# Waiting for six stores instead of 120 semaphores at the end of a kernel on SyncE

## The chip, the cores and the metric

The kernel runs on one core of one Trainium2 chip. The metric is the device time of one execution in microseconds (us). A profile of one execution goes with it: it has every instruction of the five engines, TensorE (PE), VectorE (DVE), ScalarE (ACT), GpSimd (POOL) and SyncE (SP), and the packets of the DMA engines.

## The reference

The input `x` has 2048 tokens of 512 channels. The output is a gated sum of two branches over the same input:

```
g   = sigmoid((x * gate_w).sum(-1))
a   = A(x)      # attention with a compressive memory, 32 heads, 4 segments of 512 tokens
b   = B(x)      # state-space layer: each channel convolved with its own kernel of length 2048
out = g * a + (1 - g) * b
```

Branch A projects `x` to queries, keys and values, takes causal softmax attention inside each segment, mixes it with a read from a memory that is summed up over the earlier segments, and multiplies the result by `wo`. Branch B builds, for each channel, a kernel of length 2048 from 128 complex modes and convolves the channel's 2048 values with it. The output is bf16, 2048 x 512.

## The kernel before

The kernel is a graph of operations with the order of their execution written out. `op` (line 164) records one operation with its engine, what it reads and writes, and the operations that it depends on; `dma` (line 223) records a transfer, nearly always on SyncE's queue. In the profile every plain transfer therefore has line 225, every scaled copy from PSUM line 232 or 233, and every matrix product line 706. `replay` takes the written-out order and gives each buffer (a tile) its slot in a pool; an operation that writes a slot used earlier also depends on the operations that last used the slot.

`emit` (line 267) turns this into five instruction streams. Every transfer counts a semaphore up by 16 when it has landed. There are 120 such semaphores (`NDMA` is 150, and 30 are left out), given out in turn, so that with some 257 transfers each of them is used two or three times. `emit` then goes through the operations in order and works out which waits each one needs. It keeps, for every engine, what that engine already knows: if it has waited for an operation, it knows all that this operation knew when it ran. A wait for something known is left out. `o.know` is what is known to whoever has waited for operation `o`, and `last[e]` what engine `e` knows after its last operation.

The work ends in `finals` (line 1503), which makes 16 blocks of 128 x 512 outputs. Matrix products gather both branches in PSUM; ScalarE or VectorE scales each block into half of an output tile; and every second block a transfer stores the tile, 256 KB, to the output in memory. That makes eight stores, all on SyncE, out of a pool of output tiles:

```
ouP = mkpool("ou", 2048, 6, 2)                        # line 685: six buffers
```

The pool has six buffers, so the seventh and the eighth tile take the buffers of the first and the second, and the copies that write them wait for those two stores.

When a SyncE stream has run through its operations, lines 339 to 342 add waits: one for each semaphore that any transfer has counted, to its final value. Then the block ends: each engine has a jump out of its stream and a DRAIN, and the engines meet, with GpSimd in the middle. The profile shows these under line 1603, where the block is closed.

Of the kernel before, what the change touches and what calls it, by code (L numbers as in the profile page):

```python
# [98 lines left out]
class Sched:  # L99
# [167 lines left out]
    def emit(self):  # L267
        nc, es = self.nc, self.es
        sems = {e: es.enter_context(nc.semaphore("q_" + e)) for e in ("PE", "ACT", "DVE", "POOL")}
        npool = sum(o.isdma for o in self.prog["POOL"])  # L270
        nhw = NDMA - npool if npool > 20 else NDMA - 30
        dsem = [es.enter_context(nc.semaphore("d%d" % i)) for i in range(nhw + npool)]
        block = es.enter_context(nc.Block())
        duse = [None] * len(dsem)
        dcnt = [0] * len(dsem)
        nd = nsw = 0
        last = {e: {} for e in self.prog}
        for o in self.order:
            know = dict(last[o.eng])
            o.waits = []  # L280
            deps = {id(d): d for d in o.alld}
            if o.isdma:
                if o.eng == "POOL":
                    k = nhw + nsw
                    nsw += 1
                else:
                    k = nd % nhw
                    nd += 1
                if duse[k] is not None:
                    deps[id(duse[k])] = duse[k]  # L290
                duse[k] = o
                dcnt[k] += 1
                o.sem, o.val = ("D", k), dcnt[k]
            else:
                o.sem, o.val = o.eng, o.idx
            o.inc = False
            for d in sorted(deps.values(), key=lambda d: -d.pos):
                assert d.pos < o.pos
                if d.eng == o.eng and o.eng == "PE":
                    continue  # L300
                if know.get(d.sem, 0) >= d.val:
                    continue
                o.waits.append(d)
                d.inc = True
                for kk, vv in d.know.items():
                    if know.get(kk, 0) < vv:
                        know[kk] = vv
            last[o.eng] = know
            o.know = dict(know)
            o.know[o.sem] = max(o.know.get(o.sem, 0), o.val)  # L310
        cum = {}
        for e, lst in self.prog.items():
            n = 0
            for o in lst:
                if not o.isdma and o.inc:
                    n += 1
                cum[id(o)] = n

        def tok(d):
            if d.isdma:  # L320
                return dsem[d.sem[1]], 16 * d.val
            return sems[d.eng], cum[id(d)]

        def make(e):
            def run(eng):
                for o in self.prog[e]:
                    need = {}
                    for d in o.waits:
                        s, v = tok(d)
                        if id(s) not in need or need[id(s)][1] < v:  # L330
                            need[id(s)] = (s, v)
                    for s, v in need.values():
                        eng.wait_ge(s, v)
                    ins = o.fn(eng)
                    if o.isdma:
                        ins.then_inc(dsem[o.sem[1]], 16)
                    elif o.inc:
                        ins.then_inc(sems[e], 1)
                if e == "SP":
                    for k in range(len(dsem)):  # L340
                        if dcnt[k]:
                            eng.wait_ge(dsem[k], 16 * dcnt[k])
            return run
        with nc.allow_low_precision("bf16 kernel by design"):
            block.sync(make("SP"))
            block.tensor(make("PE"))
            block.scalar(make("ACT"))
            block.vector(make("DVE"))
            block.gpsimd(make("POOL"))
# [1299 lines left out]
```

## Time and profile before

| | us |
|---|---|
| time, three runs | 289.74, 290.23, 293.19 |
| median | 290.23 |
| span of the profiled execution | 287.5 |
| busy in the span: VectorE, ScalarE, TensorE | 265.0, 254.6, 253.1 |
| last store of the output issued | 283.04 |
| waits of line 342 on SyncE: count, first and last start | 60, 283.4 and 287.0 |

The span runs from the first to the last instruction of the profiled execution. Of this execution's time the profile has no other figure than the span; the times of the table come from runs without a profile. Engines' busy times count what they compute. Instructions that only wait, jump, or issue a transfer belong to an engine's sequencer (marked q behind the engine's name) and count as nothing there; they have a start and a duration of their own all the same, and a line of the kernel. The duration of a wait instruction does not include the time that it stood waiting: its start is the time at which it could go on. A transfer is listed with the instruction that issued it, and its landing is the time at which its semaphore has its full count.

### The profile page before, as it was taken

What the parts mean: (1) busy time and instruction counts of PE and PEld (TensorE: products, weight loads), DVE (VectorE), ACT (ScalarE), POOL (GpSimd) and SP (SyncE); (2) the same over time, 40 slices, a digit from 0 to 9 for tenths busy, and PEclk for the clock granted to TensorE, in tenths of its full rate; (3) what the DMA queues carried; (4) which work ended last, traced back from release to release, by engine and by line L of the source; (5) the groups of instructions that cost most, each with busy time, mean ns of one, the idle gap of its engine ahead of it and who ended that gap; (6) DMA issues with size and microseconds to landing.
All of it is one profiled execution on the core that took longest, in us unless ns stands there. A gap on an engine that the chain in (4) does not pass through costs nothing.

```text
span 287.5 us, 9336 instructions
## 1 busy us (share of the span) xinstructions
PE 253.1 (88%) x3896; PEld 158.7 (55%) x3947; DVE 265.0 (92%) x617; ACT 254.6 (89%) x320; POOL 5.0 (2%) x10
## 2 busy tenths in 40 slices
PE   5767888787898989979999989999999999999992
PEld 2424454564556546756766657665555454555661
DVE  3998999999999999979999999999999999997782
ACT  5998999999999999989989999999999999983212
POOL 5000000000000000000000000000000000000000
PEclk9999899999999999979999999999999999999999
DMA  6996762421125256914643388585776795894224
GB/s 164 270 223 143 184 203 84 130 87 42 41 47 134 63 141 205 226 32 97 188 132 102 90 252 244 166 232 161 234 215 168 207 229 160 243 186 102 72 109 182
DMA packets 60187, 44.49 MB, mean 155 GB/s; under 512 B 36209, under 2 KB 53490, under 8 KB 60146
## 3 DMA queue, kind: packets, MB, share of 16 engines
q1 hardware_dynamic: 60146, 43.90, 57.0%
q8 instruction: 31, 0.51, 0.8%
q14 instruction: 10, 0.08, 0.1%
HBM read 22.09 MB, written 7.86 MB: 104 GB/s over the span
## 4 chain that ended last, share of the span: by engine, by line
ACT 35%; PE 28%; DVE 26%; issue 5%; DMA 3%; SPq 0%; DVEq 0%; ACTq 0%
PE psum L706 28%; ACT sb L1237 10%; ACT sb L229 10%; ACT sb L1190 8%; DVE sb L1346 7%; DVE sb L1355 3%; ACT sb L850 3%; DVE sb L230 2%; DMA sb<-sb 2%; DVE sb L1349 2%; DVE sb L1487 2%; DVE sb L1358 2%; DVE sb L1249 1%; DVE sb L1154 1%; ACT sb L1021 1%
## 5 line engine op out<-in xcount | busy, mean ns | idle before, releaser
L706 PE MATMUL psum<-sb 128*128 128x17 bf16 (+17 forms) x3808 | 247.4, 229 | 23.5 <-ACT sb L1190 7.4
L706 PEld LDWEIGHTS psum<-sb 128*128 128x128 bf16 (+6 forms) x3859 | 153.5, 102 | 115.5 <-issue 20.7
L229 ACT ACTIVATE sb<-psum 128x512 bf16<-128x512 f32 (+4 forms) x155 | 87.7, 624 | 7.6 <-PE psum L706 6.4
L1237 ACT ACTIVATE sb<-psum 128x2048 bf16<-128x2048 f32 x40 | 76.0, 1899 | 2.1 <-PE psum L706 1.7
L1190 ACT ACTIVATE sb<-psum 128x2048 bf16<-128x2048 f32 (+1 forms) x40 | 70.1, 1751 | 2.8 <-PE psum L706 2.7
L1346 DVE TENSOR_TENSOR sb<-sb 128x4096 bf16<-128x4096 bf16 (+3 forms) x24 | 37.7, 1569 | 0.0
L230 DVE CAST sb<-psum 128x512 bf16<-128x512 f32 (+1 forms) x49 | 29.9, 626 | 1.1 <-PE psum L706 0.9
L1355 DVE TENSOR_TENSOR sb<-sb 128x512 bf16<-128x512 bf16 (+1 forms) x48 | 25.0, 537 | 0.1
L1249 DVE TENSOR_TENSOR sb<-sb 128x1024 bf16<-128x1024 bf16 (+1 forms) x40 | 22.6, 577 | 0.2
L1487 DVE TENSOR_TENSOR sb<-sb 128x1024 bf16<-128x1024 bf16 x32 | 21.6, 685 | 0.9 <-ACT sb L229 0.5
L1349 DVE TENSOR_TENSOR sb<-sb 128x2048 bf16<-128x2048 bf16 (+3 forms) x24 | 20.7, 861 | 0.0
L232 ACT ACTIVATE sb<-psum,sb 128x512 bf16<-128x512 f32 x6 | 4.0, 687 | 12.3 <-PE psum L706 12.3
L1154 DVE TENSOR_TENSOR sb<-psum,sb 128x256 bf16<-128x256 f32 x32 | 13.3, 417 | 0.3
L1358 DVE TENSOR_TENSOR sb<-sb 128x512 bf16<-128x512 bf16 (+1 forms) x24 | 12.9, 536 | 0.0
L850 ACT ACTIVATE sb<-sb 128x512 f32<-128x512 f32 x18 | 11.8, 660 | 0.0
L1151 DVE RECIPROCAL sb<-psum 128x16 f32<-128x16 f32 x32 | 7.9, 252 | 1.8 <-PE psum L706 1.7
L1291 DVE TENSOR_TENSOR sb<-psum,sb 128x512 bf16<-128x512 f32 x12 | 8.2, 687 | 0.2
L858 ACT ACTIVATE sb<-sb 128x512 bf16<-128x512 f32 x12 | 8.0, 683 | 0.0
L1072 ACT ACTIVATE sb<-sb 128x512 bf16<-128x512 bf16 x12 | 8.0, 663 | 0.0
L1021 ACT ACTIVATE sb<-psum 128x512 bf16<-128x512 bf16 x12 | 7.8, 646 | 0.0
L852 DVE SCALAR_TENSOR_TENSOR sb<-sb 128x256 f32<-128x256 f32 x18 | 7.5, 424 | 0.0
L851 DVE TENSOR_TENSOR sb<-sb 128x256 f32<-128x256 f32 x18 | 7.5, 423 | 0.0
(78 smaller groups left out, 122.3 us busy)
## 6 DMA issues: line engine op xcount, KB each, us to landing
sb<-sb SPq DMA_DIRECT2D x64, 128.0 KB, 3.2
sb<-c_DN SPq DMA_DIRECT2D x32, 224.0 KB, 3.0
scr_Z<-sb SPq DMA_DIRECT2D x16, 256.0 KB, 3.2
sb<-scr_Z SPq DMA_DIRECT2D x16, 256.0 KB, 3.6
sb<-in_A_x_dram SPq DMA_DIRECT2D x5, 512.0 KB, 4.6
sb<-c_DN SPq DMA_DIRECT2D x16, 160.0 KB, 3.3
out_dram<-sb SPq DMA_DIRECT2D x8, 256.0 KB, 2.1
scr_O<-sb SPq DMA_DIRECT2D x12, 128.0 KB, 2.7
```

Source lines behind the costliest of these rows:

```text
L229: fa = lambda e: e.activation(dst(), src(), ACT.Copy)
L230: fd = lambda e: e.tensor_copy(dst(), src())
L706: mm = lambda e, o_, l, r_, st, sp, **kw: e.matmul(o_, lhsT=l, rhs=r_, start=st, stop=sp, skip_group_check=True, **kw)
L850: op("ACT", ("As", 512), lambda e, sq=sq, Z=Z: e.activation(ap(sq, n=512), ap(Z, n=512), ACT.Square), r=[Z], w=[sq], key=PW[h] + PWS * k)
L1190: o = op("ACT", ("Ax", 4 * n), lambda e: e.activation(ap(pT, dims=[[512, 4], [1, n]]), ap(P, dims=[[512, 4], [1, n]]), ACT.Exp, scale=0.25 ...
L1237: o = op("ACT", ("Ax", 2048), lambda e, P=P, pT=pT: e.activation(ap(pT, n=2048), ap(P, n=2048), ACT.Exp, scale=0.25), r=[P], w=[pT])
L1249: op("DVE", ("V2", 128 * nb), lambda e, pT=pT, dims=dims: e.tensor_tensor(ap(pT, dims=dims + [[1, 128]]), ap(pT, dims=dims + [[1, 128]]), ...
L1346: op("DVE", ("V2n1" if n == 1 else "V2", 512 * n), lambda e: e.tensor_tensor(ap(tile, 2 * dst, [[2 * (sp - dst), 2], [2 * ne, 128], [1, 2 ...
L1349: op("DVE", ("V2n1" if n == 1 else "V2", 256 * n), lambda e: e.tensor_tensor(D_(), D_(), ap(tile, 2 * sp + ne * 128, [[-ne * 128, 2], [2 * ...
L1355: op("DVE", ("V2x" if sstep > 2 else "V2", 256 * n), lambda e, half=half: e.tensor_tensor(run(t2, n, 0, 1) if half else run(tile, ne, dst, ...
L1358: op("DVE", ("V2", 256 * n), lambda e: e.tensor_tensor(D_(), D_(), ap(t2, n * 128, [[-n * 128, 2], [2 * n, 64], [1, 2 * n]]), ALU.add), r= ...
L1487: op("DVE", ("V2", 1024), lambda e, Y=Y, XAB=XAB, K3=K3, Ke=Ke, xo=xo, u=u: e.tensor_tensor(ap(Y, dims=[[512, 2], [1, 512]]), ap(XAB, xo, ...
```

## The change

After the streams are worked out, `emit` now takes what SyncE knows after its last operation and goes backwards through all transfers. A transfer whose landing SyncE does not know is put on a list, and what is known with its landing is added to what SyncE knows. The end of SyncE's stream waits for the transfers on that list, in the order in which they are issued, where it waited for every semaphore that had ever counted.

```
+        know = last["SP"]
+        tail = []
+        for d in reversed(self.order):
+            if d.isdma and know.get(d.sem, 0) < d.val:
+                tail.insert(0, d)
+                for kk, vv in d.know.items():
+                    if know.get(kk, 0) < vv:
+                        know[kk] = vv
...
                 if e == "SP":
-                    for k in range(len(dsem)):
-                        if dcnt[k]:
-                            eng.wait_ge(dsem[k], 16 * dcnt[k])
+                    for d in tail:
+                        eng.wait_ge(*tok(d))
```

Nothing else differs: the order of all operations, their engines, their buffers and their other waits are those of before.

## The prediction

> **What bounds the kernel now.** I began with the first lines of the page, to see whether one engine fills the span, and read then only its last few microseconds, because the change touches nothing before SyncE's last store.
>
> ```profile
> span 287.5 us, 9336 instructions
> PE 253.1 (88%) x3896; PEld 158.7 (55%) x3947; DVE 265.0 (92%) x617; ACT 254.6 (89%) x320; POOL 5.0 (2%) x10
> ```
>
> Three engines are busy for about nine tenths of the span. Nothing in the change makes any of their instructions shorter, so all that can move lies behind the last of them. The chain of waits, cut to the end, says which that is:
>
> ```profile
> 279.86 2.44 PE psum L706 x14
> 282.30 0.02 issue
> 282.32 0.69 ACT sb L232
> ```
>
> The chain ends with ScalarE's scaled copy of the last output block, at 282.32 + 0.69 = 283.01 us. The span ends 4.5 us later. What fills these 4.5 us is on SyncE. The order of time has the last store, and the query for the store's tensor, cut to that one store, has its landing:
>
> ```profile
> 283.04 0.33 SPq L225 DMA_DIRECT2D out_dram<-sb  x1
> L225 SPq DMA_DIRECT2D out_dram<-sb x1: 333/333/333, 283.0 to 283.0; - x1
> DMA to landing us min/median/max: 2.0/2.0/2.0
> ```
>
> The last store is issued at 283.04 and has landed 2.0 later, at 285.04 us. So I cut the end into stretches there, and asked for the waits of line 342 on either side of 285.05 (in the second fence the columns behind the count are the duration in ns, min/median/max, and the first and last start):
>
> ```profile
> 283.04:285.05 2.01, 0.00 (x0) 0.00 (x0) 0.00 (x0) 0.00 (x0) 0.00 (x0) 1.00 0.52 198
> 285.05:287.05 2.00, 0.00 (x0) 0.00 (x0) 0.00 (x0) 0.00 (x0) 0.00 (x0) 0.95 0.00 0
> 287.05:287.50 0.45, 0.00 (x0) 0.00 (x0) 0.00 (x0) 0.00 (x0) 0.00 (x0) 0.50 0.00 0
> ```
>
> ```profile
> L342 SPq EVENT_SEMAPHORE  x60: 17/28/28, 283.4 to 287.0; - x60
> L342 SPq EVENT_SEMAPHORE  x27: 17/28/28, 283.4 to 285.0; - x27
> L342 SPq EVENT_SEMAPHORE  x33: 28/28/28, 285.1 to 287.0; - x33
> ```
>
> This is the whole case. From 285.05 to 287.05 us no engine runs an instruction (x0 five times) and the DMA engines move 0 GB/s: the output is in memory, and SyncE is still stepping through 33 of its 60 wait instructions. They start evenly: 60 starts from 283.4 to 287.0 are 59 steps in 3.6 us, 61 ns each, and 33 of them make 33 x 61 ns = 2.0 us. So none of them stood waiting; each is passed at the price of an instruction. For 120 counted semaphores there are 60 instructions, which is two semaphores in each but the first, with one left for the jump out of the block. Behind the waits the end of the block follows:
>
> ```profile
> L1603 SPq COMPARE_BRANCH  x1: 41/41/41, 287.1 to 287.1; - x1
> L1603 SPq DRAIN  x1: 13/13/13, 287.3 to 287.3; - x1
> L1603 SPq EVENT_SEMAPHORE  x1: 17/17/17, 287.4 to 287.4; - x1
> L1603 PEldq EVENT_SEMAPHORE  x1: 51/51/51, 287.4 to 287.4; - x1
> L1603 ACTq DRAIN  x1: 717/717/717, 282.3 to 282.3; - x1
> ```
>
> From the jump at 287.1 to the end at 287.5 are 0.4 us, in which the engines meet. The other engines had come to their meeting point long before: ScalarE, the last, at 282.3 + 0.7 = 283.0. SyncE alone sets the end.
>
> **The change part by part.** *The waits removed.* 120 waits become six. Paired as now, six are three instructions and the one on the jump, so 57 instructions go: 57 x 61 ns = 3.5 us of SyncE's time. That is not the gain. Of the 60, 27 start while the last store is in flight, and this time stays as a wait for the store.
>
> *The wait that becomes the last.* The six stores waited for are those whose buffers nobody takes again: eight stores, six buffers in the pool, so the writers of the seventh and the eighth block have already waited for the first two stores, and SyncE knows this through its own waits for these writers. The last of the six is issued at 283.04 and sets the new end. How late can it land, and how soon does SyncE go on? The eight stores span this range, the last one in the table of stores being the slowest of them:
>
> ```profile
> L225 SPq DMA_DIRECT2D out_dram<-sb x8: 332/333/456, 275.1 to 283.0; - x8
> DMA to landing us min/median/max: 2.0/2.1/2.5
> 129.71 0.39 SPq L225 DMA_DIRECT2D scr_O<-sb  x1
> 131.70 1.13 SPq L1302 DMA_TRANSPOSE sb<-scr_O  x1
> SPq L1302 <- DMA scr_O<-sb: 1.6, 1, 1.6
> ```
>
> The first two lines bound the landing by 2.0 and 2.5 us; I take 2.0, which is this store's own value here, with nothing else in flight behind it, as will be the case again. The other three show SyncE really standing at a wait for a store: issued at 129.71, next instruction at 131.70, 1.99 us for landing and waking together. So waking adds nothing that these rows can resolve, and I allow one step of 61 ns for the instruction that waited. The jump comes at 283.04 + 2.0 + 0.06 = 285.10 in place of 287.1, which is 2.0 us sooner, or 1.5 where the landing takes 2.5.
>
> *What stays.* The other five waits of the tail are met, or nearly, when SyncE reaches them: the store before the last was issued 1.3 us earlier (281.78, in the fence below) and lands by 281.78 + 2.5 = 284.3 at the latest, before the last one does. They hide behind the last store. Without that cover they would cost two instructions, 0.12 us. Nothing is queued on SyncE behind the new wait but the jump and the meeting, 0.4 us as before.
>
> ```profile
> 281.78 0.33 SPq L225 DMA_DIRECT2D out_dram<-sb  x1
> ```
>
> *What moves.* No transfer is issued at another time and no engine's instruction is touched. The one thing that shifts is the place of the jump in SyncE's code: 57 instructions earlier. Code comes in by transfers, which the table of queues shows:
>
> ```profile
> q8 instruction: 31, 0.51, 0.8%
> q14 instruction: 10, 0.08, 0.1%
> sb<-c_sel SPq DMA_DIRECT2D x1, 6.0 KB, 2.3
> ```
>
> The smaller pieces of code are 0.08 MB / 10 = 8 KB. The jump and the DRAIN behind it stand 287.3 - 287.1 = 0.2 us apart now, so the code behind the jump is there in time. If a piece were fetched in the open, the nearest row for its price is the 6 KB load with 2.3 us to its landing. The bounds for this item are 0 and 2.3 us, and I take 0, since the 0.2 us row is the one at the very place. The Trainium skill ("Runtime: NRT & Kernel Launch", section "Instruction fetch mechanics") states that code is refilled in blocks on a queue of its own, hidden as long as it runs straight on, and that a taken jump to code outside the loaded window stalls until it is fetched. By that rule the jump could pay the fetch after the shift; by the row it pays nothing.
>
> *The sum.* The span falls from 287.5 to 285.1 + 0.4 = 285.5 us. The three runs shown are 289.74, 290.23 and 293.19; the page gives the profiled execution its span only, so between this span and the median lie 290.23 - 287.5 = 2.7 us, which I leave as they are. 290.23 - 2.0 = 288.2 us, 0.7% less. About 2% is what a measurement of this kernel can tell from no change, so this is a gain that the profile will show better than the times.
>
> **The rivals.** *The full price of the waits.* All 57 instructions would be worth 3.5 us, 290.23 - 3.5 = 286.7, if stepping through the waits also slowed the last store's landing. For it: the steps and the store do share the time from 283.4 to 285.0. Against: this store landed in 2.0 us, the least of the eight, and the stores before it had no such steps beside them.
>
> *The gain doesn't reach the time.* If what follows the span is set by something fixed, SyncE comes sooner and waits there: 290.2 us. For it: 2.7 us outside the span that no view explains. Against: all engines pass the meeting only when SyncE has, at 287.4, so whatever follows can't have begun.
>
> *The last store takes the gain in part.* With 2.5 us to its landing the gain is 1.5 us: 288.7. One store of eight had it, while others were in flight close by; the last has none behind it.
>
> *Slower: the code behind the jump comes too late.* The place is the jump at the block's end, the price 2.3 us for one piece, and it decides above 2.0 us. That gives 290.23 - 2.0 + 2.3 = 290.5. For it: the jump really moves. Against: ten such pieces in a whole span, a piece at hand now, and 2.0 us in which SyncE stands still before the jump and the piece could come.
>
> *The change does nothing.* If the known counts covered little, the list would stay long; up to 27 instructions would still be free, since so many fit beside the last store. With all 120 it is 290.2 again. The title's six and the pool's six buffers agree, so I give it next to nothing and count it with the second rival.
>
> **How the numbers follow.** Forecast 0.80, full price 0.03, gain lost in part 0.07, no gain 0.06, slower 0.04. The predicted time is 288.2. The range: downwards, the fastest run of before less 2.0 is 287.7, and 0.3 beyond that lets in the half of the way to the full price, 287.4; upwards, 288.7 for a late landing and 0.9 for the spread of runs like those shown, 289.6, which leaves no gain and slower outside. No case reaches 2% (5.8 us) either way: even all 60 waits with their 3.6 us don't. So within 2% has 0.94, and 0.03 on each side is for runs like the one at 293.19, which the rows can't explain.
>
> **What would show it.** In the profile after, the waits at the block's end should be three on SyncE where there were 60; the last store should land in 2.0 us from its issue; the jump should stand 2.05 to 2.15 us behind that issue, the DRAIN 0.2 behind the jump; and the span should end 2.5 us behind the last store's issue where it was 4.5. A jump 3 us or more behind the issue, or a wider gap from jump to DRAIN, makes the forecast wrong in the span. A span 2 us shorter with a time unchanged makes it wrong outside it. A last store issued a microsecond or more away from 283.04 would be news of the rest of the kernel, for which no row here speaks.

## The result and the profile after

| | before | after |
|---|---|---|
| median of six runs, us | 290.09 | 287.26 |
| lowest and highest, us | 289.74, 293.19 | 285.57, 290.99 |
| span of the profiled execution, us | 287.5 | 283.8 |

The ratio is 0.9887 with a 95% interval of 0.9844 to 0.9931: a gain of 1.1%, where 0.7% was forecast. The two medians are 2.83 us apart, and 287.26 lies 0.14 us below the low end of the range. (Ratios leave out the slow executions; two of the profiles further down are of such, and are used only for their last microseconds and for what lies behind their span.)

The end of the kernel went as forecast. These are rows of the changed kernel: the order of time, the landing of the last store, the waits of the new line 349, the end of the block (now line 1610), and two stretches cut at the store's issue and landing.

```profile
281.27 0.33 SPq L225 DMA_DIRECT2D out_dram<-sb  x1
DMA to landing us min/median/max: 2.0/2.0/2.0
L349 SPq EVENT_SEMAPHORE  x3: 17/28/28, 281.7 to 283.3; - x3
L1610 SPq COMPARE_BRANCH  x1: 41/41/41, 283.4 to 283.4; - x1
L1610 SPq DRAIN  x1: 13/13/13, 283.5 to 283.5; - x1
281.27:283.28 2.01, 0.00 (x0) 0.00 (x0) 0.00 (x0) 0.00 (x0) 0.00 (x0) 0.98 0.53 199
283.35:283.77 0.42, 0.00 (x0) 0.00 (x0) 0.00 (x0) 0.00 (x0) 0.00 (x0) 0.50 0.00 0
```

Three wait instructions stand where 60 stood. The last of them goes on at 283.3, 2.0 us behind the store's issue, and the span ends 283.76 - 281.27 = 2.49 us behind that issue, where it ended 4.44 behind it before: 1.95 us less. The stretch of 2.0 us in which nothing ran is gone.

The span is 3.7 us shorter, though, and the other 1.8 us lie ahead of the last store, which is issued at 281.27 and not at 283.04. No instruction there was changed. The granted clock tells the two executions apart; first the row of before, then that of after, in 40 slices each, a digit being the clock of a slice in tenths (9 is 90% or more):

```profile
PEclk9999899999999999979999999999999999999999
```

```profile
PEclk9999899999999999999999999999999999999999
```

Both have a dip in the fifth slice. The execution before has a second one in its eighteenth, from 126 us. This is the point from which the experiments start: is the gain 1.95 us and the rest a matter of which executions were compared, or does the change do more?

### The profile page after: what moved, and what is told of

Read it like the earlier page. It is cut to its first block, busy times and chain, and to the rows that moved or that the text cites. A ratio compares the mean times of both kernels' runs of the same rounds, so it can differ in the third digit from the quotient of the medians.

```text
span 283.8 us, 9330 instructions
## 1 busy us (share of the span) xinstructions
PE 258.8 (91%) x3947; PEld 157.5 (56%) x3947; DVE 265.0 (93%) x617; ACT 254.3 (90%) x320; POOL 5.0 (2%) x10
## 4 chain that ended last, share of the span: by engine, by line
ACT 43%; PE 41%; DVE 9%; issue 4%; DMA 2%; SPq 0%; ACTq 0%; DVEq 0%
PE psum L713 40%; ACT sb L1197 15%; ACT sb L229 13%; ACT sb L1244 8%; DVE sb L1353 3%; ACT sb L857 3%; ACT sb L865 2%; DVE sb L1362 1%; DVE sb L1356 1%; DMA scr_Z<-sb 1%; ACT sb L1028 1%; DMA sb<-c_ident 1%; ACT sb L1079 1%; DVE sb L1365 1%; ACT L935 0%
## 5 line engine op out<-in xcount | busy, mean ns | idle before, releaser
L713 PE MATMUL psum<-sb 128*128 128x17 bf16 (+18 forms) x3859 | 253.2, 230 | 16.4 <-ACT sb L1197 7.4
```

Of the source, the lines that this page charges most:

```text
L713: mm = lambda e, o_, l, r_, st, sp, **kw: e.matmul(o_, lhsT=l, rhs=r_, start=st, stop=sp, skip_group_check=True, **kw)
```

## The experiments

The theory (A in the expectations) was that of the prediction: 2.0 us at the end, and the rest scatter. Rival B: SyncE's shorter code also saves a fetch outside the span. Rival C: the body of the kernel runs faster after the change.

**The kernel before, again.** No edit.

> The kernel before, unchanged, run once more beside itself, so that each of its runs has its own time, span and granted clock. Theory A (the change takes 2.0 us off the end of the span; all else between two runs is scatter, half-clock stretches of TensorE among it): ratio 1.000, within 0.4%; the span ends 4.4 us behind the issue of the last store; time less span is the same 1.8 us that the runs after the change have. Rival B (SyncE's shorter code also saves a fetch of code outside the span): time less span is 2.3 to 2.7 us here. Rival C (the body of the kernel runs faster after the change): the last store is issued at 283.0 here again in runs with a granted clock of 0.993, where after the change it was 281.3.

Measured, as the ratio to the kernel before with its 95% interval, here and below: 1.0001, 0.9977 to 1.0025. Its rows, in the order span, clock, last store, waits, jump (the first profile of this kernel has 9336 instructions because the records of 51 matrix products are missing from it, 3896 in place of 3947):

```profile
span 285.6 us, 9387 instructions
PEclk9989999999999999999999999999999999999999
281.16 0.33 SPq L225 DMA_DIRECT2D out_dram<-sb  x1
L342 SPq EVENT_SEMAPHORE  x60: 17/28/28, 281.5 to 285.1; - x60
L1603 SPq COMPARE_BRANCH  x1: 41/41/41, 285.2 to 285.2; - x1
```

With one dip of the clock, the kernel before issues its last store at 281.16 us, as early as the changed kernel (281.27), and ends 4.44 us later. Rival C falls: the body of the kernel before can be as fast. Transfers that both profiles have show where the first one lost its time. First that profile, then this one: a transpose out of scratch memory, a stretch of TensorE's work (the same 47 weight loads in both, PEld), and what TensorE waited for from 118 to 131 us. The row of a stretch has its length, busy time and count on PE, PEld, DVE, ACT and POOL, the granted clock, the DMA share and GB/s:

```profile
131.70 1.13 SPq L1302 DMA_TRANSPOSE sb<-scr_O  x1
126.00:130.00 4.00, 3.96 (x53) 3.15 (x47) 3.62 (x12) 2.84 (x4) 0.00 (x0) 0.57 0.20 43
PE psum L706 <- issue: 1.7, 2, 1.5
```

```profile
129.59 1.13 SPq L1302 DMA_TRANSPOSE sb<-scr_O  x1
124.35:127.50 3.15, 2.81 (x54) 2.05 (x47) 3.15 (x11) 3.06 (x4) 0.00 (x0) 1.00 0.25 55
PE psum L706 <- issue: 0.6, 1, 0.6
```

The same transfer comes 2.1 us later in the first profile. There TensorE stood idle for 1.7 us with nothing to wait for that the profile shows (0.6 here), and then took 4.00 us, at a granted clock of 0.57, for a stretch of work that took 3.15 us at 1.00 here. That is not all of the difference: the last transfer ahead of this stretch is issued at 117.71 in the first profile and at 116.84 here, so 0.9 us had been lost earlier; the stretch adds 1.2 us, and 0.2 us are made up again before the last store, which comes 1.88 us later. Nothing in the program differs: both are the kernel before. What brings such a stretch on was not tried.

**The changed kernel, again, twice.** No edit.

> The changed kernel, unchanged, run once more. Theory A: ratio 0.993 (2.0 us of 290), the span ends 2.5 us behind the issue of the last store, time less span as in the kernel before. Rival B: ratio 0.990 to 0.991, with time less span 0.5 to 0.9 us below that of the kernel before. Rival C: ratio 0.989 again, with the last store issued some 1.3 us earlier than in runs of the kernel before with the same granted clock.

> The changed kernel once more, beside the others of this call. Theory A with the small part outside the span (2.0 us of the end, 0.25 us behind it): 2.2 us, ratio 0.992, time less span 1.8 us. If the first comparison's 0.989 was the change itself: 0.989 again.

Measured: 0.9917 (0.9892 to 0.9943) and 0.9933 (0.9894 to 0.9973). The last store was issued at 281.37 and 283.44 us, the second time with more stretches of low clock, and the span ended 2.49 us behind it both times. The kernel before had medians of 290.09, 288.25 and 289.45 us in the three sets of runs, of which the second and the third ran on two different chips: up to 1.8 us apart, nearly as much as the change is worth.

**The waits put elsewhere.** 114 of the waits are passed in SyncE's long idle stretch ahead of the first store, and six at the end:

```
+                dm = [o for o in self.prog[e] if o.isdma]
...
+                    if e == "SP" and o is dm[-8]:
+                        own = [d.sem[1] for d in dm[-8:]]
+                        for k in range(len(dsem)):
+                            if dcnt[k] and k not in own:
+                                eng.wait_ge(dsem[k], 16 * dcnt[k])
+                        for k in own[:2]:
+                            eng.wait_ge(dsem[k], 16 * (dcnt[k] - 1))
```

> The changed kernel with 114 waits that are met anyhow put on SyncE just ahead of the first store of the output, where SyncE stood idle for 7.9 us in the kernel before; six waits at the end as in the change. SyncE's code is as long as before, its end as short as after. Theory A: 57 more instructions of 61 ns, 3.5 us, all inside the idle stretch; the first store is issued when it was; ratio 0.993 and span as in the changed kernel. Rival B: the fetch comes back, time less span 2.3 to 2.7 us, ratio 0.995 to 0.996. Rival C has no reason for the body to differ from the changed kernel: 0.989, unless code length is what moves it, then 0.993.

Measured: 0.9928, 0.9902 to 0.9954.

```profile
span 283.6 us, 9387 instructions
L340 SPq EVENT_SEMAPHORE  x54: 27/28/28, 265.5 to 268.7; - x54
281.17 0.33 SPq L225 DMA_DIRECT2D out_dram<-sb  x1
L357 SPq EVENT_SEMAPHORE  x3: 17/28/28, 281.6 to 283.2; - x3
```

There are 9387 instructions again, as in the kernel before. The 57 added ones (54 of them in the row) cost the span nothing at 265 to 269 us, where the same number cost it 2 us at the end. The place is what the price hangs on. The span is that of the changed kernel; the time less the span is not, of which more below.

**Fifty waits at the end.** 44 that are met anyhow, ahead of the six:

```
+                    own = [d.sem[1] for d in tail]
+                    for k in [k for k in range(len(dsem)) if dcnt[k] and k not in own][:44]:
+                        eng.wait_ge(dsem[k], 16 * dcnt[k])
```

> The changed kernel with 44 of the waits that are met anyhow put back at the end, ahead of the six: 50 waits, 25 instructions, 1.5 us of SyncE's time. They fit into the 2.0 us of the last store's landing. Theory A: nothing is lost, ratio 0.993 as in the changed kernel, span 2.5 us behind the issue of the last store. If each wait had a price of its own beside the landing, 22 more instructions would cost 1.3 us: ratio 0.9975 and 3.8 us. Rival B: code length in between, time less span either as before or as after.

Measured: 0.9939, 0.9918 to 0.996. The last store, the added waits, the six, and the jump:

```profile
282.25 0.33 SPq L225 DMA_DIRECT2D out_dram<-sb  x1
L350 SPq EVENT_SEMAPHORE  x19: 17/28/28, 282.6 to 283.8; - x19
L352 SPq EVENT_SEMAPHORE  x6: 28/28/28, 283.8 to 284.3; - x6
L1613 SPq COMPARE_BRANCH  x1: 41/41/41, 284.3 to 284.3; - x1
```

Jump and end stand as far behind the store as with six waits (2.49 us to the end of the span). Waits that fit beside the landing are free; 0.9975, the figure for waits that cost something beside it, lies outside the interval.

**The waits gone through twice.** The loop over the kernel's 120 semaphores runs twice:

```
-                    for k in range(len(dsem)):
+                    for k in list(range(len(dsem))) * 2:
```

> The kernel before with the whole list of 120 waits at its end gone through twice: 240 waits. Theory A: 60 more instructions of 61 ns, none of them beside the store's landing any more: 3.7 us more, the span ends 8.1 us behind the issue of the last store, ratio 1.0127; time less span 2.05 us as in the kernel before. If the waits cost nothing of their own and the end came from something else: ratio 1.000.

Measured: 1.0234, 1.0157 to 1.0311. The span ends 9.13 us behind the last store, which is 4.7 us more than before and not 3.7. The last store, and then the waits: the first row is for all of them, the others for those up to 284.86, up to 288.65 and behind 289 us:

```profile
283.52 0.33 SPq L225 DMA_DIRECT2D out_dram<-sb  x1
```

```profile
L342 SPq EVENT_SEMAPHORE  x120: 17/28/28, 283.9 to 292.2; - x120
L342 SPq EVENT_SEMAPHORE  x16: 17/28/28, 283.9 to 284.8; - x16
L342 SPq EVENT_SEMAPHORE  x51: 27/28/28, 285.5 to 288.6; - x51
L342 SPq EVENT_SEMAPHORE  x53: 27/28/28, 289.0 to 292.2; - x53
```

The steps are 61 ns again (3.1 us for 51, 3.2 for 53). There are two breaks in them. The first, from 284.8 to 285.5, ends with the last store's landing: in this longer list that store's semaphore stands in the 17th instruction, so that SyncE waits there with nearly all its steps still to do. In the kernel before it stands in the 45th, at 286.1, when the store had long landed. The order is not that of the loop: the trace has the semaphores in pairs from the middle of the list outwards. The second break, of 0.4 us at 288.6, has no wait that the trace shows. It comes behind the 335th of SyncE's 391 instructions, and 1.1 us after it a piece of code is fetched (289.7); an edge between two blocks of code would fit, as will be seen, but it isn't shown.

So 3.7 us of the price is right. Of the 1.0 us that was missed, 0.65 is the order in the list, and the rest, the second break, stays open. The ratio is missed too: 1.0127 was expected, and even 4.7 us at the end give only some 1.016, at the low end of the interval. The body of the kernel was slow in the profiled one of the four executions behind it, whose last store comes at 283.52 us; the other three have no profile, and whether that is the rest isn't shown.

**The last store cut in two.** The half of block 12 goes as soon as it is ready, and the last store carries block 13 alone; the lines left out put the added store into the written-out order:

```
+            if b4 in (12, 13):
+                if b4 == 12:
+                    S.extra = len(S.ops)
+                S.dma(lambda b4=b4: bass.AP(out, b4 * 512, [[8192, 128], [1, 512]]), ..., 131072, r=[ou])
...
```

> The changed kernel with its last store cut in two: the half of block 12 is stored as soon as that block is ready, and the last store carries block 13 alone, 128 KB in place of 256 KB; seven waits at the end. Theory A says that the end is now set by the landing of the last store. If the landing follows the size, it takes some 1.5 us instead of 2.0, the span ends 2.0 us behind the last issue, ratio to the kernel before 0.9905 where the changed kernel has 0.992. If the landing is a fixed 2.0 us, the two kernels are alike; so they are if the earlier half in flight holds the last one up.

Measured: 0.992, 0.9878 to 0.9962, beside 0.9933 for the changed kernel in the same set of runs.

```profile
286.36 0.33 SPq L225 DMA_DIRECT2D out_dram<-sb  x1
DMA to landing us min/median/max: 1.8/1.8/1.8
L349 SPq EVENT_SEMAPHORE  x3: 28/28/28, 287.0 to 288.2; - x3
```

Half the bytes land in 1.8 us in place of 2.0, and the span ends 2.33 us behind the last issue in place of 2.49. Both expectations miss: the landing is neither a fixed 2.0 us nor the 1.5 us of the other, and less than 0.2 us can't be told in the times. What the size alone does stays open, because another tile's store, issued at 285.18 and landed 2.4 us later, was still in flight for 1.2 of these 1.8 us.

**What lies outside the span.** Time and span of one execution each, and the instructions of SyncE in its trace. Five more runs were made for this: the kernel before and the one with 114 waits ahead once more, the latter with 80 and with 100 waits in place of 114, and the changed kernel with 114 met waits in the idle stretch at 72 to 82 us:

```
+                dm = [o for o in self.prog[e] if o.isdma]
...
+                    if e == "SP" and o is dm[61]:
+                        for k in list(range(57)) * 2:
+                            eng.wait_ge(dsem[k], 16)
```

> The changed kernel with 80 waits that are met anyhow ahead of the first store of the output, in SyncE's idle stretch, in place of the 114 of the earlier run: SyncE's code is 40 instructions longer than in the changed kernel, 17 shorter than in the one with 114. The span as in the changed kernel in both theories. Time less span: 1.8 or 2.05 us and nothing between, with a fetch of 8 KB of code behind the span's end in the second case, if the price is that of one block of code crossed; some 1.97 us if it grows with every instruction.

> The kernel before once more, for its time less span alone. If the 0.27 us between the two kernels outside the span goes with the length of SyncE's code: 2.05 us again, with a fetch of code behind the span's end. If it was scatter: anything from 1.78 to 2.1 us.

> The kernel with 114 met waits ahead of the first store once more, for its time less span. By code length 2.05 to 2.1 us, as in the first run of it; by scatter anything from 1.78 to 2.1 us. The span ends 2.5 us behind the issue of the last store in both.

> The same with 100 met waits ahead of the first store, 50 instructions on SyncE; 40 gave 1.79 us of time less span and 57 gave 2.09. If a block's edge is crossed, 1.8 or 2.05 us, and nothing between.

> The changed kernel with 114 met waits put into SyncE's idle stretch from 72 to 82 us, 57 instructions as in the kernel before, 200 us away from the end. By code length the time less span is 2.05 us all the same, since the code at the end stands where it stood before; if what matters is work of SyncE near the end, 1.8 us. The span as in the changed kernel, 2.5 us behind the issue of the last store.

| kernel | SyncE's instructions | time | span | time less span |
|---|---|---|---|---|
| before, again | 331 | 287.65 | 285.60 | 2.05 |
| before, third profile | 331 | 287.16 | 285.16 | 2.00 |
| 114 waits ahead | 331 | 285.74 | 283.65 | 2.09 |
| 114 waits ahead, second | 331 | 288.96 | 287.06 | 1.90 |
| 114 waits at 72 us | 331 | 286.63 | 284.71 | 1.92 |
| 100 waits ahead | 324 | 287.85 | 286.04 | 1.81 |
| 80 waits ahead | 314 | 288.99 | 287.20 | 1.79 |
| fifty waits at the end | 296 | 286.53 | 284.74 | 1.78 |
| changed, first | 274 | 285.57 | 283.76 | 1.81 |
| changed, second | 274 | 285.66 | 283.87 | 1.79 |
| changed, third | 274 | 287.75 | 285.93 | 1.82 |
| last store cut in two | 275 | 290.48 | 288.68 | 1.80 |
| waits gone through twice | 391 | 294.46 | 292.65 | 1.81 |

The five with 331 instructions have 1.90 to 2.09 us outside the span, mean 1.99; the seven shorter ones 1.78 to 1.82, mean 1.80. They don't overlap, and the place of the added waits doesn't matter: those at 72 us count like those at the end. In the traces of all five, and of none of the seven, one packet of 8 KB of code moves 1.8 us behind the end of the span. First the kernel before, again, from 285.7 us on, then the changed kernel from 283.8 us on:

```profile
q14 instruction: 1, 0.01, 0.7%
DMA packets 0, 0.00 MB, mean 0 GB/s; under 512 B 0, under 2 KB 0, under 8 KB 0
```

So rival B holds in kind, and at 0.2 us where it had asked for 0.5 to 0.9. The five that pay scatter more than was expected (2.05 to 2.1), but there are more executions than those in the table, with their spans to 0.1 us. Over 59 executions of the kernel before, time less span has a mean of 2.02 us (1.75 to 2.19), over 24 of the changed kernel 1.79 (1.75 to 1.86). So the price is 0.2 us on average, while single executions scatter. It comes in one step between 324 and 331 instructions. The kernel with 240 waits is longer by far, 391, yet fetches its block inside the span, at 289.7 us, and has 1.81 us outside it: it is the place of a block's edge that counts, not the length as such. That the fetch itself costs the 0.2 us is inferred, since the two come and go together. The run with 80 waits was also timed: 0.989, 0.9823 to 0.9957, in agreement with the others.

## Why the prediction was right or wrong

**What bounds the end: right.** SyncE alone set it, in steps of 61 ns; doubling the list doubled the steps, moving them away took their price away.

**The sum: right for the span.** 2.0 us was forecast, from a landing of 2.0 us and one step; 1.95 was measured in each pair of profiles (4.44 less 2.49). The three instructions, the jump 2.1 us behind the issue and the 0.2 us to the DRAIN came as listed.

**What moves: wrong in sign.** For the shift of SyncE's code I allowed a loss of 0 to 2.3 us and took 0. The shorter code was a gain of 0.2 us outside the span, and with it went one fetch of code, as if SyncE's code now ended ahead of the edge of a block. The Trainium skill ("Runtime: NRT & Kernel Launch", section "Instruction fetch mechanics") has code coming in by blocks; the trace agrees, but the blocks on this queue (q14) are of 8 KB where the page has 16 KiB, and the fetch in question was one that the change saved, not one that it brought in the open. With it, the change is worth 1.95 + 0.2 = 2.15 us, 0.9926 of 290, which lies in the interval of all three comparisons of the changed kernel, 0.9887, 0.9917 and 0.9933.

**The range: this is the step that failed.** Its low end took the fastest of three runs, 289.74, for the floor of the kernel before, subtracted the gain and left 0.3 us to spare. That run is no floor: of the 59 later executions of the same kernel 48 were faster, down to 286.21. Executions differ by more than the change is worth, and the profile already hinted at it with a dip in the eighteenth slice of its clock row that another execution doesn't have, in a stretch that cost 1.2 us. I also put the profiled span and the median of three runs side by side and carried 2.7 us between them over as if they belonged to the kernel; by the table some 2.0 are the kernel's own, and the rest is that the median run was a slower execution than the profiled one.

From 290.23 - 2.0 down to 287.26 are 0.97 us. The median of before fell by 0.14 with three more runs; the change is worth 0.15 more than the sum's 2.0; and the other 0.7 is which executions fell into each set. That this 0.7 is scatter is argued from the repeats, not shown for those very runs, and whether such scatter ends 0.14 us inside the range or outside it is chance.

**The rivals.** The full price of the waits, 3.5 us, falls: the last store lands in 2.0 us with 27 steps beside it and with three. No gain in the time falls with the three ratios. A late landing of 2.5 us was never seen on the last store of a whole tile. Code that comes too late, 2.3 us in the open, was not seen; a fetch was at stake, as the rival had it, but with the other sign and at 0.2 us.

## What to carry to other kernels

A wait that is met already still costs its step, here 61 ns for two semaphores, and it costs time only where nothing else is left to wait for: so it is the waits at the very end that are worth pruning, down to what the last landing covers. Before a change of under 1% is sized, read the clock row of the profiled execution and split its time into span and remainder; the level of a few runs is worth less than the difference of two stretches in one trace. If the wait that is met last does not stand at the end of the list, the others are paid for after it; the order to look at is that of the trace, which need not be that of the program.

## What was not expected of the hardware

Seven instructions more or fewer on SyncE's queue, 331 in place of 324, go with some 0.2 us outside the span and with 8 KB of code fetched 1.8 us behind its end. One execution of the same program lost 1.2 us between 118 and 132 us to an idle TensorE and a granted clock of 0.57. A store of 128 KB in place of 256 landed only 0.2 us sooner, with another one still in flight beside it.
